# A decode kernel of two layers: 12 KB a partition of a V tile kept over the change of layers, weights through 26 KB in smaller pieces, and a shorter end with six w4 tiles, one transpose and one DMA

## The chip, the cores and the metric

The kernel runs on one core of a Trainium2 chip. Its time is the device time of one execution in microseconds (us). The profile is a hardware trace of one execution. Engines: PE (TensorE, matmuls), DVE (VectorE), ACT (ScalarE), POOL (GpSimd) and SP (SyncE, which here issues the DMAs). A core has 16 DMA engines. SBUF, the working memory, has 128 partitions, and sizes in KB a partition are meant in it.

## The reference

Two identical layers, each an attention block over a given cache and a mixer with an MLP. One new token for each of 2 batches; 32 heads of 128; 16384 cached keys; width D = 576; F = 4608.

```python
def _A_ref(x, k_cache, v_cache, wq, wo):
    q = (x @ wq).reshape(B, Sq, H, Dh).transpose(0, 2, 1, 3)
    scores = jnp.einsum("bhqd,bhkd->bhqk", q, k_cache) * (Dh ** -0.5)
    o = jnp.einsum("bhqk,bhkd->bhqd", _softmax(scores), v_cache)
    return o.transpose(0, 2, 1, 3).reshape(B, Sq, H * Dh) @ wo

def _B_ref(x, w1, w2, w3, w4):
    h = _gelu(_layernorm(x) @ w1)
    ...                                  # h's columns moved along the sequence
    x1 = x + hs
    return x1 + _gelu(_layernorm(x1) @ w3) @ w4

for _ in range(2):
    x = x + _A_ref(_layernorm(x), A_k_cache, A_v_cache, A_wq, A_wo)
    x = x + _B_ref(_layernorm(x), B_w1, B_w2, B_w3, B_w4)
```

Both layers read the same cache and the same weights. The cache is 2 x 64 (batch, head) tiles of 4 MB, read once a layer; the weights wq, wo, w3 and w4 are about 5 MB each.

## The kernel before

**Tiles and slots.** A unit u is one batch and head, 64 of them. Its keys are one tile K[u] of 128 partitions x 32 KB, its values V[u] another. `mem` holds six slots of 32 KB a partition, and ahead of them an area of 6 KB (AUX), which during attention holds `kt`, the transposed chunks of keys. `Store` keeps a queue of planned transfers in a fixed order: `plan` appends one with its place in `mem`, `pump` issues the queue's head as soon as all cells of its place are free, and `release` frees cells and pumps again. So transfers are issued in the planned order, by SP alone, and each waits on SP for the instruction that last used its place; what stands behind it in the queue waits with it.

**Attention.** In step s of `attention`, PE transposes half of K[u] in chunks of eight blocks (L1184), ACT copies them to `kt` (L1200), PE multiplies with q (L1210), and DVE makes the dot products of the other half (`dots`, L1240 and L1244). After the softmax PE multiplies V of the unit before (`pv`, L1300). Steps 1 to 63 are a loop of 21 turns of three. `used` releases a tile by halves once its blocks are used.

**The change of layers.** Layer 1 begins with units 63, 61 and 62, and their tiles K63, K62, K61, V63 and V62 stay in slots 1 to 5 from layer 0 (`held`). All other weights of layer 0's end (wo, w3, w4) and layer 1's wq pass through what is left: slot 0 and AUX, 38 KB a partition. `plan_all` writes down their pieces and places by hand. Their order on PE: `last_head` (the last softmax and `pv`, then `heads_projection` with wo), `two_norms`, `cols_projection` with w3, gelu, `groups_projection` with w4, `input_norm` and `cols_projection` with wq. Then V61 is loaded again into slot 0 as four parts, K0 into slot 1 as one transfer, K1 into slot 3 as two, V0 into slot 4, K2 into slot 5, and so on round the ring. In the gaps of the chain `ahead` puts transposes of K63, eight blocks each, on PE, and `lay` their copies on ACT, so that layer 1's first head has its keys transposed (`early_scores`, L1225).

**The weights.** wo comes in pieces of 8 rows of D a partition (the last in 5 and 3), w3 and wq by rows of 128 (the fifth has 64 rows, spread over 128 partitions), w4 in groups of 6, 6, 6, 6, 6, 3, 2 and 1 rows (`GROUPS`). `rows_step` (L908) multiplies a wo or w4 piece, with 5 matmuls of 128 output columns a row, the fifth overlapping the fourth since D is 4.5 x 128.

**The end.** In layer 1 all slots come free, and the weights follow V63 in the same DMA queue. After the last w4 matmul, `add_rows` adds x (two DVE operations, for the last tile has 64 partitions), `finish` transposes the five tiles of `xo` (L1316), copies 2 rows of 576 (L1319) and issues the output DMA of two rows.

Of the kernel before, what the change touches and what calls it, by code (L numbers as in the profile page):

```python
# [32 lines left out]
class Graph:  # L33
# [51 lines left out]
    def dma(self, sem, starts, reads=(), writes=()):  # L85
# [4 lines left out]
        o = Op("sync", None)  # L90
# [175 lines left out]
CELL = 128  # L266


class Store:
# [51 lines left out]

    def release(self, name, lo=0, hi=None):
# [9 lines left out]
class KB:  # L332
# [12 lines left out]
    HG = 8  # L345
    WO_CUT = 5
    PK = ["prod", "gT", "hf", "every", "y0", "y"]
    GROUPS = (6, 6, 6, 6, 6, 3, 2, 1)
    HEAD = (200, 60)

    def __init__(self, nc, A_x, K, V, wq, wo, w1, w2, w3, w4, out):
# [14 lines left out]
        assert self.BP == 64 and self.F % 128 == 0 and D == 576 and sum(self.GROUPS) == self.MT  # L366
# [16 lines left out]
    def _alloc(self):  # L383
        nc = self.nc
        sb = nc.alloc_sbuf_tensor
        B, U, KT, MT, NL = self.B, self.U, self.KT, self.MT, self.NL
# [53 lines left out]
        self.xo = sb("xo", [128, KT, B], BF16)  # L440
# [13 lines left out]
    def plan_tile(self, T, t, u, slot, parts=1, order=None):  # L454
        b, hh = u % self.B, u // self.B
        src = T[b, hh].rearrange("(p j) d -> p (j d)", p=128)
        if parts == 1:
            self.store.plan((t, u), f"tile{slot}", self.slot(slot), self.TILE, [(lambda m: m, src)])
            return
        n = self.TILE // parts  # L460
        self.parts[t, u] = parts
        for i in order or range(parts):
            self.store.plan((t, u, i), f"part{slot}_{i}", self.slot(slot) + i * n, n,
                            [(lambda m: m, src[:, i * n // 2:(i + 1) * n // 2])])
# [16 lines left out]
    def plan_heads(self, l, ats):  # L481

        D, hg = self.D, self.HG
        cuts = [(i, 0, hg) for i in range(self.ng - 1)] + [(self.ng - 1, 0, self.WO_CUT), (self.ng - 1, self.WO_CUT, hg)]
# [5 lines left out]
    def plan_groups(self, l, ats):  # L490
# [4 lines left out]
        for i, (n, at) in enumerate(zip(self.GROUPS, ats)):  # L495
            self.cuts["w4", l].append((a, a + n))
            self.store.plan(("w4", l, i), f"w4{i}", at, 2 * n * D, [
                (lambda m: m, self.w4[a * 128:(a + n) * 128, :].rearrange("(p j) n -> p (j n)", j=n))])
# [10 lines left out]
    def plan_all(self):  # L509
# [3 lines left out]
        g = [row * n for n in self.GROUPS]  # L513
# [15 lines left out]
        a, r8 = s[0], row * self.HG  # L529
        assert r8 == w3r  # L530
        self.plan_heads(0, [a, a + r8, a + 2 * r8, 0, a + 3 * r8])
        self.plan_cols("w3", 0, self.w3, [(0, 0, mt // 2, a), (0, mt // 2, mt, a + w3r // 2),
                                          full(1, mt, a + w3r), full(2, mt, a + 2 * w3r), full(4, mt, a + 3 * w3r),
# [856 lines left out]
```

## Time and profile before

| | |
|---|---|
| median of 3 runs | 2552.23 us (2552.18 to 2552.38) |
| the profiled execution | 2552.28 us, its span 2550.6 us |
| moved by DMA | 1094.77 MB, mean 429 GB/s |
| granted TensorE clock | 0.653 of full speed, 0.50 in the change of layers |
| PE / DVE / ACT busy | 60% / 74% / 44% |

How to read it: busy shares and the 40 slices tell which resource is full; the chain of waits follows the last instruction back to what released it; a stage's row gives the busy time of each engine in that stretch with its number of instructions, then the granted clock, the DMA share and GB/s. In the timeline a row is a run of like instructions: start, time from the first to the last, engine, line, operation, output and input, their number, and the idle time before with what ended it. Times of a row are from the start of the span.

### The profile page before, as it was taken

To read this page: it belongs to the slowest core of one execution; us is meant where nothing else is said; L and a number is where in the kernel's file an instruction comes from. 1 tells how busy PE (TensorE), PEld (TensorE's weight loads), DVE (VectorE), ACT (ScalarE), POOL (GpSimd) and SP (SyncE) were. 2 spreads that over 40 slices of the span, in tenths; PEclk is the share of its full clock that TensorE was granted. 3 is DMA by queue.
4 is the path that set the end of the run, shared out by engine and by line. 5 is a ranking of instruction groups with operands and counts; after the bars stand their busy time and mean duration, and the time that the engine had idled before them with its cause. 6 is when DMAs were issued, how large, how long until landed. Compare 5 with 4: busy or idle time off the path is not lost.

```text
span 2550.6 us, 75213 instructions
## 1 busy us (share of the span) xinstructions
PE 1522.6 (60%) x34456; PEld 1432.9 (56%) x34456; DVE 1888.3 (74%) x1924; ACT 1113.7 (44%) x1831; POOL 162.1 (6%) x151
## 2 busy tenths in 40 slices
PE   4655555655555565556687655655565565556556
PEld 4555555555555555555677655555555455555555
DVE  5877777777777777777649877777777777777773
ACT  3434443443444344444355544443444344344432
POOL 0000000000000000000000000000000000000000
PEclk8666666666666666666667666666666666666665
DMA  9999999999999999999999999999999999999999
GB/s 412 428 434 430 433 431 433 430 433 431 433 431 433 430 433 430 433 430 434 425 417 431 431 434 430 433 430 433 430 433 430 434 430 433 431 433 431 433 431 376
DMA packets 44900, 1094.77 MB, mean 429 GB/s; under 512 B 4922, under 2 KB 6334, under 8 KB 9662
## 3 DMA queue, kind: packets, MB, share of 16 engines
q1 hardware_dynamic: 44862, 1094.23, 100.0%
q8 instruction: 28, 0.46, 0.1%
q14 instruction: 10, 0.08, 0.0%
HBM read 1094.21 MB, written 0.00 MB: 429 GB/s over the span
## 4 chain that ended last, share of the span: by engine, by line
DMA 71%; DVE 19%; issue 8%; PE 1%; SPq 0%; POOLq 0%; DVEq 0%; ACT 0%
DMA mem<-in_A_k_cache_dram 64%; DVE s_dve L1244 9%; DVE prod L1240 9%; DMA mem<-in_A_wo_dram 3%; DMA mem<-in_B_w_dram 2%; DMA mem<-in_A_v_cache_dram 2%; DMA mem<-in_A_wq_dram 0%; DVE mx L1249 0%; PE tps L1184 0%; DVE diag L1138 0%; DVE mx L1257 0%; SPq L98 0%; DVE q_col L1129 0%; DVE o_acc L1281 0%; DVE mx L1255 0%
## 5 line engine op out<-in xcount | busy, mean ns | idle before, releaser
L1200 ACT ACTIVATE mem<-tps 128x1024 bf16<-128x1024 bf16 x1018 | 955.7, 1036 | 1290.0 <-PE tps L1184 1287.5
L1184 PE MATMUL tps<-ident,mem 128*128 128x128 bf16 x8256 | 823.3, 271 | 707.8 <-POOLq L187 707.2
L1244 DVE TENSOR_REDUCE s_dve<-prod 128x16 f32<-128x2048 bf16 x508 | 1161.3, 2286 | 17.4
L1184 PEld LDWEIGHTS tps<-ident,mem 128*128 128x128 bf16 x8256 | 677.6, 124 | 717.7 <-POOLq L187 716.8
L1240 DVE TENSOR_TENSOR prod<-mem,qb 128x2048 bf16<-128x2048 bf16 x508 | 620.6, 1222 | 527.4 <-POOLq L187 518.9
L1300 PE MATMUL mps<-p,mem 128*128 128x1 bf16 x16384 | 450.7, 165 | 85.3 <-POOLq L187 78.2
L1300 PEld LDWEIGHTS mps<-p,mem 128*128 128x128 bf16 x16384 | 443.3, 103 | 100.2 <-ACT p L1274 97.0
L1210 PE MATMUL sps<-q_col,mem 128*128 128x1 bf16 x8144 | 368.7, 167 | 159.2 <-ACT mem L1200 142.9
L1210 PEld LDWEIGHTS sps<-q_col,mem 128*128 128x128 bf16 x8144 | 320.3, 101 | 217.4 <-ACT mem L1200 212.7
L1260 POOL PARTITION_ALL_REDUCE mx<-mx x128 | 160.2, 1252 | 2331.1 <-DVE mx L1257 2331.1
L1270 ACT ACTIVATE p<-s_dve,mx 128x64 bf16<-128x64 f32 x128 | 44.5, 348 | 15.5
L1148 ACT ACTIVATE qb<-sps 128x128 bf16<-128x128 f32 x129 | 34.0, 263 | 33.5 <-PE sps L1145 33.5
L1145 PE MATMUL sps<-diag,ones_bf 128*128 128x128 bf16 x129 | 29.8, 231 | 21.6 <-DVE diag L1138 21.6
L1274 ACT ACTIVATE p<-sps,mx 128x64 bf16<-128x64 f32 x128 | 37.5, 293 | 0.0
L1268 ACT ACTIVATE mx<-mx 128x1 f32<-128x1 f32 x128 | 30.6, 239 | 14.4 <-POOL mx L1260 14.4
L1138 DVE TENSOR_SCALAR diag<-ident,q_f 128x128 bf16<-128x128 bf16 x129 | 31.6, 245 | 0.0
L1249 DVE TENSOR_REDUCE mx<-s_dve 128x1 f32<-128x64 f32 x128 | 28.2, 220 | 4.5
L835 PE MATMUL sps<-xn,mem 128*128 128x2 bf16 x544 | 21.8, 175 | 12.3 <-DMA mem<-in_A_wq_dram 6.2
L835 PEld LDWEIGHTS sps<-xn,mem 128*128 128x128 bf16 x544 | 20.7, 122 | 13.5 <-DMA mem<-in_A_wq_dram 6.8
L1255 DVE TENSOR_REDUCE mx<-sps 128x1 f32<-128x64 f32 x128 | 27.4, 214 | 0.7 <-DVEq L259 0.7
L1145 PEld LDWEIGHTS sps<-diag,ones_bf 128*128 128x128 bf16 x129 | 12.6, 97 | 22.6 <-DVE diag L1138 22.6
L1274 ACT ACTIVATION_READ_ACCUMULATOR p<-sps,mx (+1 forms) x128 | 24.2, 189 | 0.0
(115 smaller groups left out, 225.8 us busy)
## 6 DMA issues: line engine op xcount, KB each, us to landing
mem<-in_A_v_cache_dram SPq DMA_DIRECT2D x125, 4096.0 KB, 45.5
mem<-in_A_k_cache_dram SPq DMA_DIRECT2D x124, 4096.0 KB, 43.1
mem<-in_B_w_dram SPq DMA_DIRECT2D x10, 864.0 KB, 15.0
mem<-in_A_wq_dram SPq DMA_DIRECT2D x8, 1024.0 KB, 12.5
mem<-in_A_wo_dram SPq DMA_DIRECT2D x6, 1152.0 KB, 38.6
mem<-in_B_w_dram SPq DMA_DIRECT2D x6, 1152.0 KB, 16.6
mem<-in_B_w_dram SPq DMA_DIRECT2D x8, 576.0 KB, 9.3
mem<-in_A_v_cache_dram SPq DMA_DIRECT2D x4, 1024.0 KB, 8.7
```

The source lines that it names most:

```text
L835: ins = pe.matmul(out[:, m * B:(m + 1) * B], lhsT=buf[:, c:c + 127 * d + 1:d], rhs=self.xn[:, k, :], start=first and m == lo, stop=False, ...
L1145: self.pe(lambda pe: pe.matmul(qps, lhsT=self.ones_bf[:, :], rhs=self.diag[:, :], start=True, stop=True, skip_group_check=True), reads=["o ...
L1148: self.act(lambda e: e.activation(out=self.qb[s % self.NS][:, :], in_=qps, func=ACT.Copy), reads=[("qps", i)], writes=[("qb", s % self.NS) ...
L1184: ins = pe.transpose(self.tps[t][:, j * 128:(j + 1) * 128], buf[:, j * 128:(j + 1) * 128], self.ident[:, :])
L1200: self.act(lambda e: e.activation(out=self.kt[k], in_=self.tps[t][:, :].rearrange("p (i c) -> p i c", i=self.CH), func=ACT.Copy), reads=[( ...
L1210: ins = pe.matmul(self.sps[sp][:, c * self.CH + j:c * self.CH + j + 1], lhsT=self.kt[k][:, j, :], rhs=self.q_col[:, sp:sp + 1], start=True ...
L1240: self.dv(lambda e: e.tensor_tensor(out=prod, in0=buf.rearrange("p (j d) -> p j d", d=128), in1=qbc, op=ALU.mult), reads=[("qb", s % self. ...
L1244: self.dv(lambda e: e.tensor_reduce(out=sd[:, c0:c0 + DB], in_=prod, axis=AX.X, op=ALU.add), reads=["prod"], writes=[("s_dve", s % self.NS ...
L1260: self.pool(lambda e: e.partition_all_reduce(self.mx[:, 3, m:m + 1], self.mx[:, 2, m:m + 1], channels=128, reduce_op=ROP.max), reads=[("mx ...
L1270: self.act(lambda e: e.activation(out=p[:, n:self.NB], in_=self.s_dve[s % self.NS][:, :], func=ACT.Exp, bias=self.mx[:, 4, m:m + 1], scale ...
L1274: self.act(lambda e: e.activation(out=p[:, 0:n], in_=self.sps[i][:, 0:n], func=ACT.Exp, bias=self.mx[:, 4, m:m + 1], scale=self.scale, acc ...
L1300: ins = pe.matmul(self.mps[:, 448:449], lhsT=buf[:, j * 128:(j + 1) * 128], rhs=p[:, col:col + 1], start=(h == 0 and b == 0), stop=(h == 1 ...
```

## The change

V61 keeps its first 12 KB a partition over the change of layers; the window for weights is what is left, AUX and the upper 20 KB of slot 0, 26 KB. wo is cut to 4 rows a piece (8 pieces), w3 to half rows (9), w4 into groups of 5, 5, 4, 4, 5, 5, 4, 3, 1 in layer 0 (9), the last wq into two (6), each with its place in `WINDOW`. The rest of V61 comes in three parts (`REST`), K0 and K1 in four quarters each. `used` releases tiles by 16 blocks (4 KB a partition). In `last_head` `keep_o` and wo's first pieces stand ahead of `shares`, and some `ahead` and `lay` move from the norms to other gaps. w1's last 64 rows in layer 1 are one DMA instead of two. At the end, w4's columns are taken in six tiles of 96 (216 matmuls for 180, each reading 128 columns of a piece that has a gap of 128 bytes behind it), x is brought to the same form by 14 POOL copies (`recut`), and one add, one transpose, one copy and one DMA of 12 rows of 96 follow.

```diff
-    GROUPS = (6, 6, 6, 6, 6, 3, 2, 1)
+    UNIT = 16
+    GROUPS = ((5, 5, 4, 4, 5, 5, 4, 3, 1), (6, 6, 6, 6, 6, 3, 2, 1))
+    WINDOW = {
+        "wo": [0, 18432, 34304, 23040, 29696, 18432, 0, 23040],
+        "w3": [(0, 0, 34304), (0, 1, 18432), (1, 0, 23040), (1, 1, 0), (2, 0, 29696), (2, 1, 34304), (4, None, 18432), (3, 0, 0), (3, 1, 29696)],
+        "w4": [23040, 0, 28800, 33408, 18432, 0, 28800, 35456, 18432],
+        "wq": [(1, None, 20608), (2, None, 30720), (4, None, 0), (3, None, 18432), (0, 0, 34816), (0, 1, 0)],
+    }
+    PART = 12288
+    REST = [(20480, 8192), (12288, 8192), (28672, 4096)]
+    EC = 96
...
+    def rename(self, name, new, size):
+        at, _ = self.where.pop(name)
+        for c in self.cells(at, size):
+            assert self.owner[c] == name
+            self.owner[c] = new
+        self.where[new] = at, size
...
+    def partly(self):
+        return "v", self.U - self.CARRY - 1
...
         for i, (t, u) in enumerate(tiles):
-            self.plan_tile(source[t], t, u, ring[i], (4, 1, 2)[i] if i < 3 else 1, None if i else [1, 2, 3, 0])
+            q = self.TILE // 4
+            cuts = (self.REST, [(q * j, q) for j in (1, 3, 0, 2)], [(q * j, q) for j in (0, 2, 1, 3)])[i] if i < 3 else None
+            self.plan_tile(source[t], t, u, ring[i], cuts)
...
-        self.plan_small("w1", 1, self.w1, a, (0, 56, 64))
+        self.plan_small("w1", 1, self.w1, a, (0, 64))
...
     def input_norm(self, l):
...
-        self.ahead(1 - l, 2)
+        self.ahead(1 - l, 1)
...
     def two_norms(self, l):
...
-        self.ahead(l, 3)
+        self.ahead(l, 2)
...
-        self.lay(l, 4)
+        self.lay(l, 3)
...
     def between_norms(self, l):
...
+        if l == self.NL - 1:
+            self.recut()
+
+    def recut(self):
+        KT, TL = self.KT, self.TL
+        at = [(t, p) for t in range(KT) for p in range(0 if t < KT - 1 else TL, 128, 32)]
+        g = 0
+        while g < len(at):
+            (t, p), (j, q) = at[g], divmod(32 * g, self.EC)
...
+            self.pool(lambda e, t=t, p=p, j=j, q=q, n=n: e.tensor_copy(out=self.x6[q:q + 32 * n, j, :],
+                                                                      in_=self.x[p:p + 32 * n, t, :]),
+                      reads=["x"], writes=["x6"])
+            g += n
...
     def groups_projection(self, l):
...
-            if i < 3:
+            if i < 3 or i == 4:
                 self.ahead(l, 1)
-            if i < 4:
+            if i < 6:
                 self.lay(l, 1)
...
+        m = self.EC
+        self.tt(self.xo[0:m, :, :].rearrange("p b t -> p t b"), self.x6[0:m, :, :],
+                self.mps[0:m, 0:self.ET * self.B].rearrange("p (t b) -> p t b", b=self.B), ALU.add,
+                ["x6", "mps"], ["xo"])
...
     def last_head(self, l, s, u):
...
-        self.ahead(l, 1)
+        self.ahead(l, 2)
         self.softmax_exp(s)
...
-        self.shares(first, U)
-        self.keep_o(s, None)
-        self.heads_projection(l, 0)
+        self.keep_o(s, None)
+        for i in range(n[0]):
+            self.heads_projection(l, i)
+        self.shares(first, U)
         self.normed(l, first, U)
+        for i in range(n[0], n[1]):
+            self.heads_projection(l, i)
         self.dealt(late, U, self.sps[0], ("sps", 0), self.masked[1], self.oB[:, :], "oB")
-        self.heads_projection(l, 1)
...
     def used(self, l, t, u, b0, n):
...
+                if l == 0 and (t, u) == self.partly() and lo < self.PART:
+                    continue
+                self.store.release((t, u), lo, lo + step)
...
+        if l == 0 and whole and (t, u) == self.partly() and b0 + n == self.NB:
+            self.store.rename((t, u), (t, u, 0), self.PART)
...
     def finish(self):
...
-            for t in [KT - 1] + list(range(KT - 1)):
-                c = self.kcol[t]
-                ins = pe.transpose(mb[0:B, c:c + 128], self.xo[:, t, :], self.ident[:, :])
+        m, n = self.EC, self.ET * B
+        self.pe(lambda pe: pe.transpose(mb[0:n, 0:m], self.xo[0:m, :, :].rearrange("p b t -> p (b t)"),
+                                        self.ident[0:m, 0:m]), reads=["xo", "ident"], writes=["mps"])
+        rows = self.rows[0:n, 0:m]
+        self.dv(lambda e: e.tensor_copy(out=rows, in_=mb[0:n, 0:m]), reads=["mps"], writes=["prod"])
+        o = g.dma("out", [(self.out.rearrange("b s (t c) -> (b s t) c", c=m), rows)], reads=["prod"])
```

More of the change, by code (lines that the diff above doesn't have):

```diff
@@ L89, in dma @@
             self.dma_count[sem] = 0
[L90 removed]
+        o = Op(eng, None)
         o.sem = sem
@@ L365, in __init__ @@
         self.BP = self.NB // 2
-        assert self.BP == 64 and self.F % 128 == 0 and D == 576 and sum(self.GROUPS) == self.MT
+        assert self.BP == 64 and self.F % 128 == 0 and D == 576 and all(sum(x) == self.MT for x in self.GROUPS)
         self.KT = (D + 127) // 128
@@ L512, in plan_all @@
         row, w3r, wqr = 2 * D, 2 * self.F, 2 * 128 * self.H
-        g = [row * n for n in self.GROUPS]
+        g = [row * n + CELL for n in self.GROUPS[1]]
         self.cuts, self.korder = {}, {}
@@ L815, in block_cols @@
         a = 0
-        for n in self.GROUPS:
+        for n in self.GROUPS[l]:
             if m < a + n:
@@ L1118, in landed @@
         nm = t, u
-        names = [nm] if nm in self.store.where else [(t, u, i) for i in range(self.parts[nm])]
+        names = [nm] if nm in self.store.where else [(t, u, lo) for lo in self.parts[nm][1]]
         keys = [k for x in names for k in self.store.keys(x)]
```

126 lines of the change are left out of this document (64 added, 62 removed).

## The prediction

> **What bounds the kernel now.** I read the page's engine shares and slices first, then its chain of waits, then the stages around the change of layers.
>
> ```profile
> span 2550.6 us, 75213 instructions
> PE 1522.6 (60%) x34456; PEld 1432.9 (56%) x34456; DVE 1888.3 (74%) x1924; ACT 1113.7 (44%) x1831; POOL 162.1 (6%) x151
> DMA  9999999999999999999999999999999999999999
> DMA packets 44900, 1094.77 MB, mean 429 GB/s; under 512 B 4922, under 2 KB 6334, under 8 KB 9662
> DMA 71%; DVE 19%; issue 8%; PE 1%; SPq 0%; POOLq 0%; DVEq 0%; ACT 0%
> ```
>
> No engine is busy over three quarters of the span, yet the DMA row is full in all 40 slices. The bytes set the time, so a saved byte is worth its transfer, if no hole in the transfers takes it back. Holes can only come where the window for weights is small: the change of layers.
>
> ```profile
> 1190.00:1250.00 60.00, 35.16 (x800) 32.75 (x798) 45.68 (x46) 27.10 (x45) 3.76 (x3) 0.66 1.01 434
> 1260.00:1310.00 50.00, 39.57 (x880) 36.92 (x879) 8.82 (x54) 18.47 (x27) 0.00 (x0) 0.50 1.01 414
> 1310.00:1360.00 50.00, 41.11 (x964) 38.86 (x965) 44.49 (x48) 29.43 (x47) 3.76 (x3) 0.71 1.01 421
> 1360.00:1400.00 40.00, 28.50 (x666) 26.41 (x664) 38.60 (x41) 24.27 (x41) 3.76 (x3) 0.75 1.00 432
> ```
>
> The last two columns are the DMA share and GB/s. Before, even the change of layers (1260 to 1310) has a share of 1.01: 38 KB a partition are enough. It runs at 414 GB/s instead of 432.
>
> ```profile
> q1 hardware_dynamic: 3698, 20.97, 99.8%
> q8 instruction: 7, 0.11, 0.9%
> mem<-in_B_w_dram SPq DMA_DIRECT2D x5, 864.0 KB, 8.9
> ```
>
> This is the list of DMA queues for 1259 to 1310. Seven packets of 16 KB bring instructions; 0.9% of 16 engines in 51 us is 7.3 us, or 1.05 us each, and for that long one of the 16 DMA engines moves nothing of ours.
>
> **The change part by part.**
>
> *The V tile.* 12 KB a partition are 12288 x 128 = 1.573 MB that are not read again: at 432 GB/s **-3.64 us**.
>
> *More pieces.* wo goes in 8 pieces instead of 5, w3 in 9 for 7, w4 in 9 for 8, wq in 6 for 5; then V in 3 for 4, K0 in 4 for 1, K1 in 4 for 2: 11 more. At the end, w1's tail is one DMA instead of two (9 KB; nothing). At 414 instead of 432, 50 us lose 2.08 us; the seven instruction packets explain 7 x 1.05 / 16 = 0.46; the remaining 1.62 us over some 25 pieces is 0.065 us a piece, and 11 pieces are **+0.7 us** (0.3 to 1). SP spends about 0.33 us on an issue and holds nothing else, so its own time is hidden as long as the queue is filled.
> The Trainium skill's page "DMA: Bandwidth & Descriptors", section "Anatomy of one DMA — SWDGE (gpsimd) path", gives each DMA about 2.0 us of fixed cost. By that rule 11 pieces would be 22 us; the rows give 0.065 us a piece in a full queue, and something like it only at an empty queue, next.
>
> *The smaller window: 26 KB instead of 38.* A piece may be issued when the piece that lay in its place is consumed. I follow each such link: from the landing of the releasing piece to the first bytes of the next, against the work that is still queued behind the releasing piece. The start of an empty queue shows the price from issue to bytes:
>
> ```profile
> 0.79 0.39 SPq L98 DMA_DIRECT2D mem<-in_A_k_cache_dram  x1
> 0.00:20.00 20.00, 2.97 (x72) 2.60 (x72) 1.98 (x12) 2.97 (x4) 1.95 (x23) 1.00 0.91 372
> ```
>
> 20 us at 372 are 17.2 us at 432; less the 0.79 before the first issue, 2.0 us were lost (bounds 1.5, if the small pieces' own rate is counted, and 2.5). The consumers:
>
> ```profile
> 1262.80 3.55 PE L1300 MATMUL mps<-p,mem 128*128 128x1 bf16 x128 [1.55 <-POOLq L187]
> 1267.07 1.21 PE L908 MATMUL sps<-oA,mem 128*128 128x2 bf16 x40
> 1274.01 0.56 PE L908 MATMUL sps<-oB,mem 128*128 128x2 bf16 x15
> 1275.76 2.74 PE L1184 MATMUL tps<-ident,mem 128*128 128x128 bf16 x24
> 1278.37 3.25 PE L835 MATMUL sps<-xn,mem 128*128 128x2 bf16 x72
> 1285.38 1.00 PE L835 MATMUL sps<-xn,mem 128*128 128x2 bf16 x18
> 1286.78 0.89 PE L835 MATMUL sps<-xn,mem 128*128 128x2 bf16 x18 [0.40 <-DMA mem<-in_B_w_dram]
> 1289.05 0.96 PE L908 MATMUL mps<-prod,mem 128*128 128x2 bf16 x30 [0.50 <-DVE prod L1000]
> 1299.12 0.65 PE L908 MATMUL mps<-prod,mem 128*128 128x2 bf16 x15 [0.18 <-DMA mem<-in_B_w_dram]
> 1302.61 0.99 PE L835 MATMUL sps<-xn,mem 128*128 128x2 bf16 x32
> ```
>
> And from the chain of waits, issue and time to landing of the last pieces of wo, w4 and wq:
>
> ```profile
> 1253.31 20.66 DMA mem<-in_A_wo_dram
> 1290.04 9.03 DMA mem<-in_B_w_dram
> 1299.58 10.93 DMA mem<-in_A_wq_dram
> ```
>
> At 414 GB/s a piece of 4608 bytes a partition takes 1.42 us, 5760 1.78, 8192 2.53, 4096 1.27, 1152 0.36.
> (a) wo's sixth piece needs the second consumed: 1262.80 + 3.55 + 1.21 + 0.05 = 1267.6, bytes at 1269.6. The last V landed just before 1262.80, and five pieces behind it last 7.1 us, to 1269.8. To spare: 0.2.
> (b) w3's third needs the last wo: 0.56 + 0.1 + 2.0 = 2.66 against two pieces, 2.84. To spare: 0.2.
> (c) w3's sixth needs its first consumed, past the norm: from the landing at 1253.31 + 20.66 = 1273.97 to 18 matmuls after 1278.37, 5.3, less 0.2 because 16 transposes stand there instead of 24, plus 2.05 = 7.15 against five pieces, 7.1. Short by 0.05.
> (d) w4's second needs a piece of w3: 1.0 + 2.05 against 1.42 + 1.78. To spare: 0.15.
> (e) w4's fifth needs its first, past gelu: 1.0, then 1289.05 - (1286.78 + 0.89) = 1.4, 25 matmuls 0.8, and 2.05, together 5.25 against 6.4. To spare: 1.15.
> (f) wq's second needs w4's last but one: 0.65 + 2.05 against 0.36 + 2.53. To spare: 0.2.
> (g) wq's fourth needs its first, past the norm. The last w4 lands some 0.3 after 1290.04 + 9.03, wq's first is consumed at 1302.61 + 0.99 = 1303.6: 4.2 + 2.05 against 2.53 + 2.53 + 1.27 = 6.33. To spare: 0.1.
>
> So seven links hold by some tenths each. Before, 12 KB more were queued at each of them, 1.573 MB or 3.8 us. That reserve paid for instruction packets: a piece has landed when the last of 16 engines has delivered, and an engine held for 1.05 us delays one landing by as much, which the reserve swallowed. Without it the delay, less some 0.15 to spare, reaches the next link, where the other 15 engines run dry. Seven such packets fall into this stage, about one a link; (e) swallows its own, (a) comes when the first is past, and one may meet an engine that waits anyway. Four of seven: 4 x 0.9 = **+3.6 us**, between 0.4 (all hidden; only short links pay) and 7 x 1.05 = 7.4.
> The Trainium skill's page "Runtime: NRT & Kernel Launch", section "Instruction fetch mechanics", says that fetches come in 16 KiB blocks over a queue of their own and that their cost is mostly hidden. The size agrees with the row; hidden they are in a stage with reserve, and by the rule the sum would be the first rival's.
>
> *The first heads of layer 1.* Here the V tile is missing as cover. K2 needs head 62 finished by DVE:
>
> ```profile
> 1331.90 0.33 SPq L98 DMA_DIRECT2D mem<-in_A_v_cache_dram  x1
> mem<-in_A_v_cache_dram SPq DMA_DIRECT2D x1, 4096.0 KB, 19.2
> 1345.52 0.22 DVE L1249 TENSOR_REDUCE mx<-s_dve 128x1 f32<-128x64 f32 x1
> ```
>
> wq's last piece lands at 1299.58 + 10.93 = 1310.51. DVE frees K2's place 35.2 later, with 2.0 to the bytes 37.2; the last piece is now half as large, -0.5: 36.7. The transfers last until 1331.90 + 19.2 = 1351.1, 40.6 after wq; without 3.64 they last 37.0. They still cover DVE, by 0.3: cost 0, and the cutting of K0 and K1 into quarters only brings their issue forward. Were that cover gone, each tenth would show.
>
> *The end.*
>
> ```profile
> 2546.70 0.67 PE mps L908 x15
> 2547.39 0.17 DVE xo L596
> 2547.59 0.17 DVE xo L596
> 2547.80 0.71 PE mps L1316 x5
> 2548.54 0.45 DVE prod L1319
> ...
> 2523.86 0.17 DVE L596 TENSOR_TENSOR st<-st,x 128x10 f32<-128x10 f32 x1
> ...
> 2549.01 0.27 SPq L98 DMA_DIRECT2D out_dram<-prod  x1
> ...
> L1260 POOL PARTITION_ALL_REDUCE mx<-mx x128 | 160.2, 1252 | 2331.1 <-DVE mx L1257 2331.1
> ```
>
> Two adds become one (-0.2), five transposes one (0.71 to about 0.25), the copy shrinks from 576 to 96 elements a partition (0.45 to about 0.18), the 15 matmuls become 18 (+0.1). An output DMA of 12 rows of 192 bytes instead of 2 of 1152 has no row; from its issue to the end of the span are 1.6 us in all, few of them data, so its extra is bounded by 0 and 0.3, and I take 0: both move 2.3 KB. Together **-0.8 us**. The 36 extra matmuls of w4 (about 1.2 us at 0.032) lie in PE's waits for w4. POOL's 14 copies of x have no row: between 0.17 each, as a small DVE operation above, 2.4 us, and 1.25 each, as POOL's one large operation, 17 us. They begin once x is final (2523.86 is the add that makes it), and the add that needs them waits for the last w4 landing, over 20 us later: hidden either way. What DVE might lose beside them lies behind w3's and w4's transfers. In last_head the matmuls of the sums (shares) now stand behind wo's first pieces on PE, which is in (a).
>
> *Sum.* -3.64 + 0.7 + 3.6 - 0.8 = -0.1. The profiled execution took 2552.28 (span 2550.6 and 1.7 around it); the median shown is 2552.23, 0.05 less. Predicted: **2552.1 us**, no change.
>
> **The rivals.**
> 1. *The window suffices.* Instruction packets stay hidden, the links pay 0.4: 2552.28 - 3.64 + 0.7 + 0.4 - 0.8 = **2548.9**. For it: the links' own sum is not negative. Against: nearly nothing is to spare, and 16 engines must all deliver.
> 2. *The window costs more than the V tile saves* (the other side). Links (a) to (g), each 0.3 short once issue to bytes is 2.5, 5 x 0.3 = 1.5, and five packets in place of four, 5.25: 2552.28 - 3.64 + 0.7 + 6.75 - 0.8 = **2555.3**. It decides as soon as the holes add up to over 3.7 us. For it: six links within 0.2 of empty.
> 3. *The change does not save what it says.* DVE sets the first heads: the 3.64 us become a wait before K2. 2552.28 + 0.7 + 3.6 - 0.8 = **2555.8**. Against: 37.0 over 36.7.
> 4. *Each of the 11 pieces costs the 2.0 us of the empty queue*, serially: 2552.28 - 4.44 + 22 = **2569.8**. Against: 0.065 a piece. The Trainium skill's page "DMA: Bandwidth & Descriptors" has such a fixed cost in the section named above.
>
> **How the numbers follow.** Forecast 0.40 (2550.3 to 2554), rival 1 0.28, rival 2 0.26, rival 3 0.05, rival 4 0.01. The range reaches from rival 1 nearly to its lower end (holes at 0, pieces at 0.3: 2548.1) past rivals 2 and 3: **2548.6 to 2556.2**; the forecast's own is 2550.3 to 2554. 0.2% is 5.1 us, about what a measurement of this kernel can tell from no change: below 2547.1 only rival 1 with a better end, 0.03; above 2557.3 the upper half of rival 2's bounds and rival 4, 0.07; within, 0.90.
>
> **What would show it.** Right: GB/s of the change of layers below 414 with a DMA share under 1; wq's last landing some 4 us later than 1310.5 against the last PV; a tail from the last w4 matmul to the end shorter by 0.8. Rival 1: share still 1.0, wq later by no more than 0.6. Rival 3: a hole before K2 near 1350. Wrong altogether: the end moved by over 5 us, or holes in layer 0's loop, which the change doesn't touch.

## The result, and the profile after

The changed kernel takes 2561.28 us (median of 6 runs, 2559.91 to 2563.94) against 2552.20 (2551.95 to 2552.38): the ratio is 1.0037, 95% interval 1.0024 to 1.005. It is slower by 9.1 us, outside the predicted range. Its runs also scatter by 4 us, where those of the kernel before scatter by 0.4. The profiled execution took 2560.13, with a span of 2558.3, so the two profiles lie 7.85 us apart.

The page of the changed kernel: span, DMA share and GB/s in 40 slices, and the queue of data.

```profile
span 2558.3 us, 75293 instructions
DMA  9999999999999999999999999999999999999999
GB/s 411 432 428 433 434 429 433 433 429 433 433 429 433 433 429 433 432 430 433 397 365 424 431 432 432 431 432 432 431 432 432 431 433 432 430 433 432 430 433 386
q1 hardware_dynamic: 46460, 1092.66, 99.8%
```

The bytes are really saved: 1092.66 MB, where a kernel that reads all of head 61 moves 1094.23 (the row is shown with e6). The row of busy shares still shows nines everywhere. The GB/s under it do show the place: slices 20 and 21, the change of layers, have 397 and 365. The same stages as in the prediction, last two columns DMA share and GB/s:

```profile
1190.00:1250.00 60.00, 35.07 (x795) 32.53 (x793) 45.72 (x46) 27.15 (x45) 3.75 (x3) 0.66 1.01 433
1260.00:1310.00 50.00, 34.07 (x750) 30.84 (x747) 8.96 (x54) 16.81 (x25) 0.00 (x0) 0.50 0.92 340
1310.00:1360.00 50.00, 39.63 (x908) 38.15 (x908) 33.61 (x37) 26.68 (x41) 2.50 (x2) 0.62 0.99 386
1360.00:1400.00 40.00, 29.14 (x686) 27.94 (x684) 38.59 (x40) 21.12 (x37) 3.76 (x3) 0.65 1.00 431
```

Up to 1250 nothing is changed. From 1260 to 1310 the rate falls from 414 to 340 GB/s, and the share only from 1.01 to 0.92: packets take longer then and still count as busy (one of 4608 bytes took 206 ns on average between 1266 and 1300 in this trace, 182 before the change). After 1360 all is as before. So the loss lies between 1260 and 1325. The chain of waits there (start, length, what) names its form:

```profile
1269.58 6.60 DMA mem<-in_A_wo_dram
1276.23 0.57 PE sps L953 x15
...
1277.19 5.88 DMA mem<-in_B_w_dram
1283.11 0.81 PE sps L879 x18
1283.94 6.07 DMA mem<-in_B_w_dram
1290.05 0.84 PE sps L879 x18
1290.91 5.63 DMA mem<-in_B_w_dram
...
1300.78 5.34 DMA mem<-in_B_w_dram
1306.16 0.59 PE mps L953 x17
1306.75 6.15 DMA mem<-in_A_wq_dram
...
1315.27 6.72 DMA mem<-in_A_wq_dram
```

Before, this stretch had four transfers on the chain, with norms and gelu between. Now seven short links follow one another: a piece is issued, lands 5.3 to 6.7 us later, PE reads it in 0.6 to 1.0, and that frees the place of the next. wq's last piece lands at 1315.27 + 6.72 = 1321.99, 11.5 us later than the 1310.51 of before.

### The profile page after: what moved, and what is told of

The parts are those of the page before. It is cut to its first block, busy times and chain, and to the rows that moved or that the text cites. A ratio compares the mean times of both kernels' runs of the same rounds, so it can differ in the third digit from the quotient of the medians.

```text
span 2558.3 us, 75293 instructions
## 1 busy us (share of the span) xinstructions
PE 1523.3 (60%) x34486; PEld 1434.5 (56%) x34486; DVE 1888.1 (74%) x1923; ACT 1114.9 (44%) x1831; POOL 164.4 (6%) x163
## 3 DMA queue, kind: packets, MB, share of 16 engines
q1 hardware_dynamic: 46460, 1092.66, 99.8%
## 4 chain that ended last, share of the span: by engine, by line
DMA 70%; DVE 19%; issue 9%; PE 1%; SPq 0%; POOLq 0%; DVEq 0%; ACT 0%
DMA mem<-in_A_k_cache_dram 64%; DVE s_dve L1301 9%; DVE prod L1297 9%; DMA mem<-in_B_w_dram 3%; DMA mem<-in_A_wo_dram 2%; DMA mem<-in_A_v_cache_dram 1%; DMA mem<-in_A_wq_dram 1%; SPq L98 0%; DVE mx L1306 0%; PE tps L1241 0%; DVE diag L1190 0%; DVE mx L1314 0%; DVE q_col L1181 0%; DVE o_acc L1338 0%; DVE mx L1312 0%
## 5 line engine op out<-in xcount | busy, mean ns | idle before, releaser
L1338 DVE COPY o_acc<-mps 128x1 f32 (+1 forms) x130 | 19.3, 149 | 8.4 <-PE mps L1357 8.4
## 6 DMA issues: line engine op xcount, KB each, us to landing
mem<-in_A_k_cache_dram SPq DMA_DIRECT2D x8, 1024.0 KB, 10.2
```

## The experiments

Theory W, formed on this profile: the window of 26 KB costs the time, because a queue that is nearly empty costs more than the forecast's 2.0 us from issue to bytes. The rivals: the smaller pieces cost it wherever they lie, the new end costs it, or the V tile's saving does not arrive.

### Where the loss lies: e1, e2, e6

**e1** is the kernel before with the new end alone:

```diff
-        self.add_rows(self.xo[:, :, :] if last else self.x, "xo" if last else "x", self.mps, "mps")
+        self.tt(self.xo[0:m, :, :].rearrange("p b t -> p t b"), self.x6[0:m, :, :],
+                self.mps[0:m, 0:self.ET * self.B].rearrange("p (t b) -> p t b", b=self.B), ALU.add,
+                ["x6", "mps"], ["xo"])
...
+        self.pe(lambda pe: pe.transpose(mb[0:n, 0:m], self.xo[0:m, :, :].rearrange("p b t -> p (b t)"),
+                                        self.ident[0:m, 0:m]), reads=["xo", "ident"], writes=["mps"])
```

> The kernel before with the new end alone (w4 in six tiles of 96, one add, one transpose, one copy, 12 rows of output; nothing else of the change). Theory W (the loss of the change lies in its 26 KB window, at the change of layers): the end is worth what the forecast gave it, -0.8 us, so 2551.4 us against 2552.2. Rival E (part of the loss lies at the end, since POOL's 14 copies or the 12 short rows cost more than their rows said): 2552.2 or more.

Measured: 2551.64 us (2551.25 to 2552.02) against 2552.36, so -0.72 (ratio 0.9998, 0.9988 to 1.0007). The end of its chain of waits:

```profile
2546.84 0.68 PE mps L934 x18
...
2547.61 0.20 DVE xo L600
...
2547.86 0.26 PE mps L1345
...
2548.14 0.20 DVE prod L1348
```

The output is issued after it, in its timeline:

```profile
2548.37 0.34 SPq L98 DMA_DIRECT2D out_dram<-prod  x1
```

From the last 18 matmuls to the output's issue are 2548.37 - 2546.84 = 1.53 us; before they were 2549.01 - 2546.70 = 2.31. The difference of 0.78 is the forecast's sum (one add less, one transpose of 0.26 for five of 0.71, a copy of 0.20 for 0.45), and it arrives nearly whole in the time. The end is no part of the loss.

**e2** is the changed kernel with the window of before, all 38 KB, and V head 61 read again as a whole (the places of wo, w3 and wq change like those of w4):

```diff
-    PART = 12288
-    REST = [(20480, 8192), (12288, 8192), (28672, 4096)]
+    PART = 0
+    REST = [(8192, 8192), (16384, 8192), (24576, 8192), (0, 8192)]
...
-        return "v", self.U - self.CARRY - 1
+        return None
...
-        "w4": [23040, 0, 28800, 33408, 18432, 0, 28800, 35456, 18432],
+        "w4": [10752, 16512, 22272, 26880, 31488, 0, 5760, 10752, 37760],
```

> The changed kernel with the window of before: all 38 KB a partition for the weights, V head 61 read again as a whole, but the smaller pieces, the quarters of K0 and K1 and the new end kept. Theory W: no link runs dry, wq's last landing is back within 1 us of 1310.5, and the time is 2552.28 + 0.7 - 0.8 = 2552.2 (2551.4 to 2553). Rival P (the pieces themselves cost it, about 1 us for each of the 11 that came in): the 11.5 us by which wq's last landing is late stay, and with 3.64 us of V read again the time is 2561.3 + 3.6 = 2564.9. A time between, near 2556, would split the loss between pieces and window.

Measured: 2556.06 (2555.76 to 2557.02): between the two, and the reason is a fault of this kernel's own. The stretch from 1290 to 1300 in its profile:

```profile
1290.00:1300.00 10.00, 6.80 (x141) 6.45 (x138) 0.90 (x6) 5.57 (x7) 0.00 (x0) 0.50 0.66 250
```

One hole with a share of 0.66. The piece at 5760 shares a 2 KB cell with the piece at 0 (the store follows the first 6 KB in cells of 2 KB), so it was issued only when that one had landed. **e6** moves it:

```diff
-        "w4": [10752, 16512, 22272, 26880, 31488, 0, 5760, 10752, 37760],
+        "w4": [10752, 16512, 22272, 26880, 31488, 0, 6144, 10752, 37760],
```

> The wide window of e2 with one piece of w4 moved off a 2 KB cell that it shared with the piece before it; there it waited for that piece's landing, and one hole of some 4 us at 1297 followed. Theory W: 2556.1 - 4 = 2552 (2551.5 to 2552.8), the pieces' price being under 1 us in all. Rival P (the 11 pieces cost 4 us wherever they lie): 2556.

Measured: 2553.04 (2552.89 to 2553.41; ratio to the kernel before 1.0002, 0.9993 to 1.0012), 8.2 us under the changed kernel though it moves 1.57 MB more. Its stage by windows, the last piece of wq on its chain of waits, and its queue of data:

```profile
1260.00:1310.00 50.00, 37.84 (x878) 34.80 (x878) 8.97 (x54) 18.60 (x28) 0.00 (x0) 0.53 1.01 403
```

```profile
1301.74 9.96 DMA mem<-in_A_wq_dram
```

```profile
q1 hardware_dynamic: 46604, 1094.23, 100.0%
```

wq's last piece lands at 1311.70, 10.3 us earlier than in the changed kernel, with the same pieces and the same order of work. So neither is the loss: e6 lies 1.40 us over e1, which has the same end and the old pieces. That is their price in all, twice the forecast's 0.7 and more than its upper bound of 1; it also put e6 just over the 2552.8 that theory W allowed.

### How much window is enough: e3, e7, e8, e4

e3 and e7 keep 8 KB of the V tile (window 30 KB), e8 keeps 4 KB (34 KB). The pieces are those of the changed kernel, at places that leave as much as possible queued at each link (e8's are shown). In e3 two pieces share a 2 KB cell, as in e2; in e7 and e8 none do.

```diff
-    PART = 12288
+    PART = 8192
...
-    PART = 12288
+    PART = 4096
...
+        "wo": [1536, 10240, 14848, 19456, 34304, 24064, 384, 28672],
+        "w3": [(0, 0, 10240), (0, 1, 14848), (1, 0, 19456), (1, 1, 34304), (2, 0, 1536), (2, 1, 28672), (4, None, 24064), (3, 0, 10240), (3, 1, 14848)],
+        "w4": [384, 33152, 19456, 24064, 13696, 0, 33280, 28672, 10240],
+        "wq": [(1, None, 20480), (2, None, 12288), (4, None, 2048), (3, None, 29696), (0, 0, 24576), (0, 1, 20480)],
```

> The changed kernel with 8 KB of the V tile kept instead of 12, a window of 30 KB, the same pieces at other places. Theory W: 4 KB more queued at each link are 1.27 us. The late landings of the changed kernel (1.8, 0.7, 0.5, 1.3, 1.5, 0.6, 1.3, 2.0 and 0.8 us against pieces landing one behind the other) shrink by as much each, to 1.5 us in sum: 2552.28 - 2.43 + 0.7 - 0.8 + 1.5 = 2551.3 (2550 to 2553). Rival P (pieces): 2561.3 + 1.2 = 2562.5. A loss that fell only in proportion, by a third, would be 2561.3 + 1.2 - 3.8 = 2558.7.

> 8 KB kept, window 30 KB, with places in which no two pieces share a 2 KB cell (in e3 two did: a hole near 1295). Theory W: every link has at least 4 us from the releasing landing to the moment the queue is empty: 2552.3 - 2.43 - 0.72 + 0.7 = 2549.9 and up to 1.5 of holes: 2550 to 2551.4. Rival: 30 KB lose as e3 did, 2553.3.

> 4 KB kept, window 34 KB, the same pieces. Theory W: no link runs dry, 2552.3 - 1.21 - 0.72 + 0.7 = 2551.1 (2550.5 to 2551.6). A loss in proportion to what is kept (9 us for 12 KB) would give 2551.1 + 3 = 2554.

Measured: e3 2553.28 (2552.05 to 2555.53), e7 2554.19 (2551.09 to 2555.51), e8 2551.49 (2550.92 to 2552.06). e7's mending brought nothing that its scatter would show, and its expectation missed by some 3 us; e8 came as expected. The stage by windows and the last piece of wq on the chain, of e7 and then of e8:

```profile
1260.00:1310.00 50.00, 37.77 (x846) 34.76 (x846) 9.46 (x56) 19.14 (x30) 0.00 (x0) 0.50 1.00 392
```

```profile
1305.59 7.63 DMA mem<-in_A_wq_dram
```

```profile
1260.00:1310.00 50.00, 38.66 (x878) 35.74 (x878) 9.17 (x55) 18.85 (x29) 0.00 (x0) 0.50 1.01 405
```

```profile
1304.40 6.85 DMA mem<-in_A_wq_dram
```

Set against e6, with each kept byte counted at 432 GB/s (1.21 us for 4 KB), the window costs:

| window | kernel | time, us | without a loss: 2553.04 less the V bytes | lost | wq's last landing |
|---|---|---|---|---|---|
| 38 KB | e6 | 2553.04 | 2553.04 | 0 | 1311.70 |
| 34 KB | e8 | 2551.49 | 2551.83 | -0.3 | 1311.25 |
| 30 KB | e3, e7 | 2553.28, 2554.19 | 2550.61 | 2.7, 3.6 | 1313.22 (e7) |
| 26 KB | changed | 2561.28 | 2549.40 | 11.9 | 1321.99 |

The last row holds what the first heads of layer 1 give back (below) as well. The loss is not in proportion to what is kept: the first 4 KB cost nothing, the second 3 us or so, the third 8 to 9 more. The scatter of the runs comes with it: 1.1 us at 34 KB, 4.4 in e7, 4.0 at 26.

The traces also show what is left in the queue. Counted from the issue of each piece to its last landing, between 1270 and 1305 us, 29 KB a partition are on their way on average before the change, 28 in e6, 23 in e8, 21 in e7, 19 in e3 and 15 in the changed kernel (3.3 pieces). Fewer than 18 KB, a mark that e9 gives below, are on their way for none of that time before and in e8, for 3% of it in e6, 14% in e7, 21% in e3 and 63% in the changed kernel. The loss goes with this share.

**e4** takes the V tile's saving away and leaves the window of 26 KB:

```diff
-    PART = 12288
-    REST = [(20480, 8192), (12288, 8192), (28672, 4096)]
+    PART = 0
+    REST = [(0, 12288), (20480, 8192), (12288, 8192), (28672, 4096)]
```

> The changed kernel, window and pieces as they are, but V head 61 read again as a whole: 12 KB a partition more, as a fourth piece of the tile whose place is free from the start. It prices the saving alone. If the saving is whole: 2561.3 + 3.64 = 2564.9. If the first heads of layer 1 took some of it back (between wq's last landing and K3's the changed kernel was 2.1 us shorter, not 3.64): 2561.3 + 2.1 = 2563.4. If DVE sets the first heads (rival 3 of the prediction) and nothing was saved: 2561.3.

Measured: 2564.77 (2560.08 to 2565.34, 4 runs), 3.5 us over the changed kernel. That looks like the whole saving, but both scatter by 4 to 5 us, and in its profile wq's last piece lands at 1324.22, already 2.2 us late by the window alone. The medians don't tell 3.64 from 2.1. The profile speaks for 2.1: K3 lands 69.8 us after wq's last piece (1373.89 + 20.1 - 1324.22), against 67.7 in the changed kernel (below); that is one execution of each.

### The price of a short queue: e5, e9, e16

**e5** moves pieces of w3 alone, with one, two or three places in turn, each with PE idle and then with PE running matmuls without a loop:

```python
for bufs in (1, 2, 3):
    for busy in (0, 1):
        if busy:
            pe_run(1500, ["mem0"])
        for i in range(24):
            b = i % bufs
            ...
            g.dma(f"p{bufs}{busy}{b}", [(mem[:, b, :], w3[k * 128:(k + 1) * 128, h * 2304:(h + 1) * 2304])],
                  reads=reads, writes=[f"mem{b}"])
```

> Not the reference's computation: only pieces of 4608 bytes a partition (halves of rows of w3, 1.42 us at 414 GB/s) and a zero output. Six stretches of 24 pieces: one piece at a time (each is issued when the last of 16 engines has landed the one before), two places in turn, three places in turn, each once with PE idle and once with PE running matmuls without a loop, whose instructions have to be fetched. The forecast's price, 2.0 us from issue to bytes: one at a time 3.4 us from issue to the last landing with PE idle, and up to 1.05 more in the stretch with PE running for the pieces that meet a fetch. Theory S (at an empty queue the 16 engines don't start together, and the last lands 1 to 3 us after the first, fetches or not): 4.5 to 6 us with PE idle as well, and little more with PE running. Theory F (the fetches are what makes the last engine late): 3.4 us idle, over 4.4 on average with PE running.

The six stretches by windows (columns PE, PEld, DVE, POOL, clock, share, GB/s), and, from the list of DMA issues, the median time to landing with one, two and three places, PE idle:

```profile
0.00:90.00 90.00, 0.00 (x0) 0.00 (x0) 0.41 (x2) 0.20 (x4) 1.00 0.51 157
90.70:181.00 90.30, 85.30 (x1499) 85.12 (x1497) 0.00 (x0) 0.00 (x0) 0.99 0.51 159
181.00:236.00 55.00, 0.00 (x0) 0.00 (x0) 0.00 (x0) 0.00 (x0) 0.50 0.79 252
236.30:296.00 59.70, 59.70 (x1035) 59.70 (x1033) 0.00 (x0) 0.00 (x0) 0.96 0.78 242
322.00:365.00 43.00, 0.29 (x5) 0.13 (x3) 0.00 (x0) 0.00 (x0) 0.55 0.88 313
365.20:414.00 48.80, 48.80 (x832) 48.80 (x831) 0.00 (x0) 0.00 (x0) 0.95 0.88 306
```

```profile
mem<-in_B_w_dram SPq DMA_DIRECT2D x24, 576.0 KB, 3.7
...
mem<-in_B_w_dram SPq DMA_DIRECT2D x24, 576.0 KB, 4.8
...
mem<-in_B_w_dram SPq DMA_DIRECT2D x24, 576.0 KB, 5.6
```

One piece at a time takes 3.7 us, 2.3 more than its 1.42 of transfer: the forecast's 2.0 to 2.5 was right there, and theory S's 4.5 to 6 wrong. But with three places each issue comes while 2.84 us of work are queued, more than 2.3, and still only 313 GB/s move. Issue to landing is then 5.6 us, where 2.84 + 1.42 = 4.26 would be the transfers alone. Theory F falls too: where PE ran and instructions were fetched (7 to 12 packets a stretch), the times to landing are the same 3.7, 4.8 and 5.6 us, and the rates are 159 for 157, 242 for 252, 306 for 313 (in the middle of the stretches, without start and end, 157 for 156, 247 for 254, 311 for 317).

**e9** asks how many bytes must be on their way: the same loop, PE idle, with

```python
for size, bufs in ((4608, 4), (4608, 5), (4608, 6), (4608, 8), (2304, 4), (2304, 6), (2304, 8), (9216, 2), (9216, 3)):
```

> Not the reference's computation: pieces of w3 alone and a zero output, PE idle, 24 pieces a stretch, each issued when the piece before it in its place has landed. In the first price kernel one place moved 157 GB/s, two 252, three 313. The forecast's rule (2.0 us from issue to bytes; nothing is lost when more work than that is queued) would have had 414 from three places on. Theory S (issue to the landing of the last of 16 engines is 2.3 us plus the piece plus about 2 us by which the engines stand apart): 4608 bytes a partition in 4 places 370 to 400, 5 places 400 or more, 6 and 8 places full, 414 and over. 2304 bytes: 8 places as 4 of 4608 or a little better, since places come free in smaller steps; 4 places 240 to 280. 9216 bytes: 2 places 320 to 350, 3 places full. Rival (a price for each piece, whatever is queued): 6 and 8 places stay under 380.

Of its nine stretches, in that order, the middle of the first and of the fourth to the eighth, without start and end (columns DVE, POOL, clock, share, GB/s):

```profile
5.00:35.00 30.00, 0.00 (x0) 0.00 (x0) 1.00 1.02 412
...
116.00:146.00 30.00, 0.00 (x0) 0.00 (x0) 1.00 1.02 414
152.00:170.00 18.00, 0.00 (x0) 0.00 (x0) 1.00 0.91 310
180.00:190.00 10.00, 0.00 (x0) 0.00 (x0) 1.00 1.03 382
203.00:211.00 8.00, 0.00 (x0) 0.00 (x0) 1.00 1.05 399
220.00:282.00 62.00, 0.00 (x0) 0.00 (x0) 1.00 1.01 418
```

Over whole stretches the same rows are 377, 387, 284, 327, 332 and 402. Those contain start and end, and since the stretches are 21 to 70 us long, they can't be compared with one another.

Four places of 4608 bytes (18 KB) reach 412 of the 414 GB/s that eight reach; three places had 317 in e5, two 254, one 156. For pieces of 4608 an issue that comes 2.84 us before the queue is empty is so too late, and 4.26 us are enough; the forecast had 2.0. The expectation was right in this, and wrong on the sizes. At the same 18 KB on their way, two pieces of 9216 do better than it said (418), though each is issued with only 2.84 us queued. Of 2304 bytes, eight places (18 KB) move 399, a little less than four of 4608, and six (14 KB) 382, more than three of 4608 with as many bytes. So with 18 KB on their way each size came to 399 or more, while the time that is queued is no common measure for them.

**e16** puts the larger pieces of before into the window of 26 KB:

```diff
-    GROUPS = ((5, 5, 4, 4, 5, 5, 4, 3, 1), (6, 6, 6, 6, 6, 3, 2, 1))
+    GROUPS = ((6, 6, 6, 6, 6, 3, 2, 1), (6, 6, 6, 6, 6, 3, 2, 1))
...
-        "wo": [0, 18432, 34304, 23040, 29696, 18432, 0, 23040],
+        "wo": [29696, 20480, 29696, 384, 20480],
...
-        "wq": [(1, None, 20608), (2, None, 30720), (4, None, 0), (3, None, 18432), (0, 0, 34816), (0, 1, 0)],
+        "wq": [(1, None, 29696), (2, None, 18432), (4, None, 2048), (3, None, 29696), (0, None, 18432)],
...
-        self.plan_heads(0, w["wo"], 2)
+        self.plan_heads(0, w["wo"])
```

> The changed kernel's window of 26 KB with the larger pieces of before (wo in 5, w3 in 7, w4 in 8, wq in 5). Theory W (bytes on their way decide: a place stays taken until the whole piece has been read, so larger pieces leave fewer bytes on their way in the same window): slower than the changed kernel's 2561.3, between 2566 and 2572. Rival (in a short queue larger pieces move faster, 402 GB/s with two of 9216 against 377 with four of 4608 and 313 with three, and 7 pieces fewer save some 0.7 us): 2555 to 2560.

Measured: 2563.37 (2562.49 to 2564.22), 2.1 us over the changed kernel, between the two expectations. Its stage:

```profile
1260.00:1310.00 50.00, 33.13 (x741) 30.84 (x741) 7.28 (x43) 15.78 (x25) 0.00 (x0) 0.50 0.84 318
```

The rate is lower still. So the smaller pieces don't cause the loss; by the medians they take 2 us off it, less than theory W gave them, and the runs of the two kernels overlap. In e16's trace 13 KB are on their way on average. With either cut the window of 26 KB sets the loss.

### The first heads of layer 1: e10 to e15

Between wq's last landing and K3's the changed kernel should be 3.64 us shorter. K3's issue in the timeline of the changed kernel and its time to landing in the list of issues, then both for e6:

```profile
1371.68 0.33 SPq L98 DMA_DIRECT2D mem<-in_A_k_cache_dram  x1
```

```profile
mem<-in_A_k_cache_dram SPq DMA_DIRECT2D x1, 4096.0 KB, 18.0
```

```profile
1362.07 0.33 SPq L98 DMA_DIRECT2D mem<-in_A_k_cache_dram  x1
```

```profile
mem<-in_A_k_cache_dram SPq DMA_DIRECT2D x1, 4096.0 KB, 19.8
```

1389.7 - 1322.0 = 67.7 against 1381.9 - 1311.7 = 70.2: 2.5 us shorter. About 1.1 of the 3.64 are given back here. K2 shows a part of it. The issues of V0 and K2 in the changed kernel, and their times to landing:

```profile
1342.50 0.68 SPq L98 DMA_DIRECT2D mem<-in_A_v_cache_dram  x1
1356.87 0.33 SPq L98 DMA_DIRECT2D mem<-in_A_k_cache_dram  x1
```

```profile
mem<-in_A_v_cache_dram SPq DMA_DIRECT2D x1, 4096.0 KB, 17.1
...
mem<-in_A_k_cache_dram SPq DMA_DIRECT2D x1, 4096.0 KB, 13.3
```

V0 lands at 1359.6 and K2 at 1370.2, 10.6 later, where 4 MB at 432 GB/s take 9.7. K2 was issued 2.7 us ahead of V0's landing. Theory D is that this wait for DVE takes back part of the V tile's saving. It can't be the whole: V0 itself landed 10.9 after K1 (1348.7), though it was issued 6 us before that.

**e10** (on the changed kernel) and **e11** (on e8) issue V1 ahead of K2, which was meant to give K2 more cover:

```diff
-            self.plan_tile(source[t], t, u, ring[i], cuts)
+            cuts_of.append((source[t], t, u, ring[i], cuts))
...
+        cuts_of[4:6] = cuts_of[5], cuts_of[4]
+        for x in cuts_of:
+            self.plan_tile(*x)
```

> The changed kernel with one exchange in the order of issue: V1 ahead of K2 in layer 1. V1's place comes free with PV of head 61, K2's some 3.6 us later with DVE's last pass over head 62. Theory D (the saved V bytes uncovered K2's issue: between wq's last landing and K3's the changed kernel won 2.1 us, not 3.64): the wait goes, 2561.3 - 1.5 = 2559.8. Rival (K2's issue is covered and the rest went elsewhere): 2561.3, or slower if K2's bytes, now 9.7 us later, come too late for DVE.

> 4 KB kept (e8) with V1 issued ahead of K2. Theory D: in e8 K2 was issued 0.55 us before the first engine had finished V0, and 10.0 us instead of 9.7 passed between the two landings; with the wait gone 2551.5 less 0.3 to 1.2: 2550.3 to 2551.2. Rival (covered): 2551.5.

Measured: 2561.16 (2559.76 to 2565.15) and 2551.64 (2550.99 to 2553.05), nothing won. The premise was wrong: e10's SP issues V0 and V1 in the first row and K2 in the second,

```profile
1341.68 14.19 SPq L98 DMA_DIRECT2D mem<-in_A_v_cache_dram  x2
1356.01 15.18 SPq L98 DMA_DIRECT2D mem<-in_A_k_cache_dram  x2
```

and V1's issue, the last 0.3 us before 1355.87, is only 0.5 ahead of K2's. Its place came free no earlier, so nothing was tested.

**e12** (changed kernel), **e13** (e8) and **e14** (e1) read K2 in halves; **e15** is e13 with K0 whole and K1 in halves, five pieces fewer:

```diff
-            cuts = (self.REST, [...], [(q * j, q) for j in (0, 2, 1, 3)])[i] if i < 3 else None
+            cuts = (self.REST, [...], [(q * j, q) for j in (0, 2, 1, 3)], None, [(0, 2 * q), (2 * q, 2 * q)])[i] if i < 5 else None
...
+            cuts = (self.REST, None, [(0, 2 * q), (2 * q, 2 * q)], None, [(0, 2 * q), (2 * q, 2 * q)])[i] if i < 5 else None
```

> The changed kernel with K2 read in two halves, so that its first half can be issued when DVE has done the first half of head 62, some 7 us before the rest. Theory D (K2's issue, 34.9 us after wq's last landing, comes when the first engines have finished V0, and takes back part of the V tile's 3.64 us): K2 lands 9.7 us behind V0 instead of 10.6, wq to K3 takes 66.2 to 66.8 us instead of 67.7, and the time falls by about 1, to 2560.3 (its runs scatter by 4). Rival (the rest went elsewhere): 67.7 and 2561.3 stay.

> 4 KB kept (e8) with K2 in halves. Theory D: wq to K3 takes 68.9 us instead of 69.3, 2551.5 - 0.4 = 2551.1 (2550.3 to 2551.4). Rival: 2551.5, or up to 0.2 more for one more piece.

> The kernel before with the new end (e1) and K2 in halves, nothing kept: here V head 61 still covers K2's issue on the last engine (9.7 us from V0's landing to K2's). Theory D: nothing to win, 2551.6 (2551.4 to 2551.8). If it wins 0.4 or more, halves help for another reason and e12 and e13 don't speak for theory D.

> As e13, with K0 whole and K1 in halves as before the change, four pieces... five fewer. If the quarters of K0 and K1 have a part in the 1.4 us that the wide window with small pieces (e6) lies over e1, this saves 0.3 to 0.6: 2550.6. If the pieces in the window are all of it: as e13, 2551.1.

Measured: e12 2562.02 (2558.14 to 2563.31), e13 2551.60 (2551.10 to 2552.00), e14 2551.54 (2551.34 to 2551.95), e15 2551.14 (2550.64 to 2553.97). In e12 the first half of K2 is issued 28.5 us after wq's last landing (1323.7) instead of 34.9, and the second behind it in one row of the timeline,

```profile
1352.24 7.78 SPq L98 DMA_DIRECT2D mem<-in_A_k_cache_dram  x2
```

but wq to K3 stays at 67.7 us, and the time is no shorter; in e13 wq to K3 falls by 0.3 of theory D's 0.4 and the time not at all. K2 does land sooner behind V0 (10.2 us instead of 10.6 in e12, 9.8 instead of 10.0 in e13), but in e12 two quarters of K0 land 0.8 and 1.1 us late instead. So theory D is not borne out: an earlier K2 wins no time. What holds the first heads of layer 1 stays open; it is about a tenth of the loss. e15 against e13 is -0.46: by the medians the quarters of K0 and K1 are about a third of the pieces' 1.40; the runs of the two overlap.

e15 is the shortest of all, 1.25 us (0.05%) under the kernel before in its median. Its interval of the ratio, 0.9987 to 1.0005, doesn't part it from no change.

## Why the prediction was wrong

| term | forecast | measured | from |
|---|---|---|---|
| V tile | -3.64 | -3.64 | the bytes, 1094.23 to 1092.66 MB |
| 11 more pieces | +0.7 | +1.4 | e6 - e1 |
| the smaller window | +3.6 | +10.3 | wq's last landing, 1321.99 against e6's 1311.70 |
| the first heads | 0 | +1.1 | wq to K3, 67.7 against 70.2 - 3.64 |
| the end | -0.8 | -0.72 | e1 |
| sum | -0.1 | +8.4 | the two profiles: +7.85; the medians: +9.1 |

The terms of the window and of the first heads come from one profiled execution of each kernel.

*The step that failed* is the price in the window: "the price from issue to bytes" of 2.0 us, taken from the start of the kernel, and with it the rule that a link holds when that much work is queued behind the releasing piece. By it the forecast put the links' own loss at nothing (0.4 in rival 1). The price itself is right for a queue that is empty anyway (2.3 in e5). As a reserve it is too small: with pieces of 4608 and 2.84 us queued e5 moved 317 GB/s, and e9 reached 412 of 414 only with 4.26 us queued. Links (a) to (d), (f) and (g), which had "to spare" between -0.05 and 0.2, were by this measure all between 0.6 and 2.3 us short. An estimate from these rows: at 317 instead of 414 GB/s a piece of 0.59 MB takes 1.86 instead of 1.42 us, and 32 pieces lose 14; the window lost 10.3. Three pieces on their way is about what 26 KB leave (3.3 in the trace), since the place of a piece stays taken from its landing until PE has read it. What the runs show in place of the forecast's +3.6 is the curve of the loss over the window and over the bytes on their way, and that neither the pieces (e6, e16) nor the end (e1) make it.

*What the price hides.* A piece has landed when the last of 16 engines has delivered it, and its place comes free then. The engines that are ahead run dry earlier. In the trace's landing records the first and the last engine deliver the same piece 0.4 to 0.9 us apart in e5 with one place (once 1.8), mostly 1.2 to 2.9 apart with three, and 3.3 to 3.4 apart for wo's first pieces, before the change as after it. The forecast said that "16 engines must all deliver", but gave only the engine that an instruction packet holds a delay, and counted the queue from the last landing. In e9 the engines land a piece of 9216 only 0.35 us apart (median, two places), and in e5 one of 4608 1.8 apart (three places), both with 2.84 us queued behind it. The engine that is ahead so has 2.5 us of work left in the one and 1.0 in the other, where the price at an empty queue is 2.3; the first reaches its full rate and the second doesn't. Whether the engines drift apart first or the queue runs short first, no run shows. The Trainium skill's page "DMA: Bandwidth & Descriptors", section "Latency and other measured facts", has an HBM access latency of 0.2 us on average and 2 us at high load. No run here shows that latency by itself: the time from issue to landing grows from 3.7 us with one piece on its way to 5.6 with three, but up to 2.84 of the 5.6 are the wait behind the two pieces ahead.

*The instruction packets* carried the forecast's +3.6. e5 shows rates 2 to 3% lower with PE running at two and three places (middle of the stretches), and no lower at one: an estimate for 50 us of window is 1 to 1.5 us. So that term was oversized, and the links' own loss undersized far more.

*The list of links* was not the chain. Of the seven that the profile has, those of wo at 1269.58, w3 at 1283.94, w4 at 1300.78 and wq at 1315.27 stand for pieces that (a) to (g) don't name. When most of the queue is gone, nearly every piece is a link.

*The pieces.* 0.065 us each became 0.13. The forecast's bounds, 0.3 to 1, were too narrow; that this is no price of 2.0 us a piece (rival 4) is shown by e6. The section of the Trainium skill's page "DMA: Bandwidth & Descriptors" that rival 4 names is on DMAs that GpSimd issues; here SP issues them.

*The first heads.* "They still cover DVE, by 0.3: cost 0" did not hold: 1.1 us of the saving are missing there (1.5 by e4's profile). That K2's issue takes them, as rival 3 would have it, e12 and e13 did not confirm.

*The end* was right in each part. POOL's copies of x are 13, not 14, of 0.18 us each, the lower of the two bounds, and hidden:

```profile
L818 POOL COPY x<-st 32x2 f32<-32x2 f32 (+2 forms) x13 | 2.3, 179 | 19.7 <-DVE st L619 18.9
```

*The rivals.* Rival 2 had the right sign and place, and its rule of decision ("as soon as the holes add up to over 3.7 us") held. Its price, 6.75 us of holes, came from latency 2.5 and five packets, and so from the same step. Of the signs named to look for, a rate under 414 with a share under 1 and the shorter tail came as said; wq's last landing was late by 11.5 instead of 4. The Trainium skill's page "Runtime: NRT & Kernel Launch", section "Instruction fetch mechanics", calls the cost of a fetch mostly hidden. It says so of the engine that fetches; for the transfers beside it e5's 2 to 3% are the measure here.

## What to carry to other kernels

A buffer that is refilled as it is read needs enough bytes on their way at any moment to reach the full rate: here 18 KB a partition were enough, in pieces of 4.5 and 9 KB, and 14 KB in pieces of 4.5 were not, beside what is being read. Below that the loss is steep (none at 34 KB of window, 3 us at 30, 12 at 26), and a sum over links with one fixed latency misses it. Before memory is taken from such a window, measure the rate with two, three and four pieces on their way, or give the memory up in small steps.

## What the runs showed of the hardware that was not expected

- A DMA share near 1 doesn't mean a full rate: 0.92 went with 340 GB/s in the window, where 414 moved before, and 0.90 with 317 in the middle of e5's stretch of three places, where more places moved 414 in e9.
- With 14 KB a partition on their way, six pieces of 2304 bytes moved 382 GB/s and three of 4608 only 317; with 18 KB, eight, four and two pieces of 2304, 4608 and 9216 moved 399, 412 and 418.
- The small windows went with uneven runs as well: 4 us between runs of the changed kernel, 1.1 with 34 KB (e8), 0.4 before.
